# Reordering the end of a sliding-window attention and soft-MoE kernel: products, a spread and sums moved between the last products, results copied by two engines, first outputs of one token

## The chip, the cores and the metric

The kernel runs on one core of a Trainium2 chip. The core has five engines that run their own instruction streams and meet through semaphores: TensorE (PE, with its weight loads as PEld), VectorE (DVE), ScalarE (ACT), GpSimd (POOL) and SyncE (SP). Data moves between HBM and SBUF through 16 DMA engines, which all queues share. Matmul results land in PSUM, 8 banks of 512 fp32 columns in each partition. The metric is device time in microseconds, the median of several executions; a profiled execution also gives a span and a trace.

## The reference

Attention over a causal window of 64 positions, for 8 batches, 8 heads, 576 positions and head size 64, gives `x` (4608 tokens of 512 columns). A soft mixture of experts follows, with 8 experts of 4 slots each:

```python
logits = x @ phi                          # 4608 x 32
d = softmax(logits, axis=0)               # over the tokens
slot_input = (d.T @ x).reshape(8, 4, 512)
h = relu(slot_input[e] @ w1[e])           # 512 -> 1024, for each expert e
slot_out[e] = h @ w2[e]                   # 1024 -> 512
c = softmax(logits, axis=1)               # over the 32 slots
out = c @ slot_out                        # 4608 x 512, fp32
```

## The kernel before

The order of all work is written out by hand (`tc.manual_schedule()`): each engine executes its instructions in the order of the program text, and the framework adds the semaphore waits that the data and the buffers need. Attention is computed in 32 steps of two heads. While it runs, the dispatch softmax is accumulated, and the weights are loaded and cast by transfers on the GpSimd queue. The outputs go out through transfers on SyncE's queue.

What the change touches is the end, from about 147 us on.

- `first` (L871) and `turn_hidden` (L886) compute the hidden layer of the experts in two groups of four: group 0 is experts 0 to 3, group 1 experts 4 to 7. `second_first` (L893) multiplies group 0 by its second weights into one PSUM bank, `op`, over all 512 columns.
- For group 1 the 512 output columns are done in two halves, `d` = 0 and 1, of `DH` = 256 columns. `second(d)` (L899) adds experts 4 and 5, whose weights are there early; `second_last(d)` (L906) adds experts 6 and 7. The weights of experts 6 and 7 are loaded last, half by half (`load_half`, L165): for each `d`, two transfers of expert 6 (tile `w`) and then two of expert 7 (tile `w2h`), each with four of the eight chunks `fc`. `j` = 2 is expert 6 and `j` = 3 expert 7.
- The result of a half is copied from `op` to SBUF, to `osb` (shown by its buffer's name, `qb`), and is then the moving operand of the output products.
- The combine weights of each batch lie in `ct_all` in a compact form. `spread(b, copy)` (L716) widens them: five products into the PSUM tile `rp`, then one copy of 576 columns to `ct4` (shown as `v`) by the engine given. `ct4[k]` holds batches 2k and 2k+1. `sums(k)` (L731) makes the softmax denominators of `ct4[k]` by nine products, again into a tile `rp`, and VectorE writes their reciprocals, `rcs`. The pool `psr` has one buffer for `rp`, so a spread or sums waits until the reader of the `rp` before is done.
- `give(k, e0, ne, c0, nc_)` (L951) makes one piece of output: for the batches 2k and 2k+1, of the 9 tokens that each partition holds, those from `e0` to `e0+ne`, and the columns `c0` to `c0+nc_`. For each token there is one product into a PSUM tile `cp` (L961), and then one scaled copy into an SBUF buffer `ob`, by ScalarE (L968) or VectorE (L966). A `cp` is one bank: two tokens of 256 columns or one of 512, with 4 buffers in the pool `pst`. The counter `turn` goes up by one for each tile `cp`, so that the two engines take whole tiles in turn. At the end the piece is issued as one transfer on SyncE (L970). There are 7 buffers for pieces.
- `fill(k, bank)` issues `k` products of 512 columns whose results nobody reads.

The output order is: left half (columns 0 to 255) of batches 0 to 3, right half of the same, and then whole rows of the other four batches, three tokens to a piece. After `second(0)` the program issues `spread(2, act)`, `second_last(0)`, the copy of the first half by ScalarE, the products of `spread(3)`, the pieces `give(0, 0, 2)` and `give(0, 2, 2)`, the copy of `spread(3)` by VectorE, `give(0, 4, 5)`, `second(1)` and `sums(1)`, and so on.

Of the kernel before, what the change touches and what calls it, by code (L numbers as in the profile page):

```python
# [9 lines left out]
FP32 = mybir.dt.float32  # L10
# [8 lines left out]
def kernel(  # L19
# [13 lines left out]
    D, NSLOT = moe_phi.shape  # L33
# [129 lines left out]
    DH = D // 2  # L163
# [13 lines left out]
    def w2_at(e, d, fc):  # L177
        return w2_t[e][d][fc] if e == last else w2_t[e][fc][:, DH * d:DH * d + DH]
# [367 lines left out]
    def cb_exp(b):  # L546
        ec = pw.tile([128, 6, 32], FP16, name="ec", tag="ec") if b < B - 1 else \
            lh[:, 3:5, :].rearrange("p i x -> p (i x)")[:, 0:192].rearrange("p (i s) -> p i s", s=32)
        nc.scalar.activation(ec[:, :, :], lgs.pop(b)[:, :, :], AF.Exp)
        cbs[b] = ec  # L550

    def cb_turn(b):
        nc.vector.transpose(ct_all[:, b, :], cbs.pop(b)[:, :, :].rearrange("p i s -> p (i s)"))
# [138 lines left out]
    def fill(k, bank):  # L692
        for _ in range(k):
            nc.tensor.matmul(bank, ident_h[:, :], wm[:, 0:4, :].rearrange("p c x -> p (c x)"),
                             start=True, stop=True, skip_group_check=True)
# [15 lines left out]
    def spread(b, copy, rp=None):  # L711
        if rp is None:
            rp = psr.tile([128, 1024], FP32, name="rp", tag="rp")
        for t in range(5):
            w = 128 if t < 4 else 64
            nc.tensor.matmul(rp[:, 128 * t:128 * t + w], ss4[:, min(t, 3), :],  # L716
                             ct_all[:, b, 128 * (t // 4):128 * (t // 4) + w], start=True, stop=True,
                             skip_group_check=True)
        copy(out=ct4[b // 2][:, :, 64 * (b % 2):64 * (b % 2) + 64],
             in_=rp[:, 0:S].rearrange("p (x e) -> p e x", e=NE))  # L720
# [7 lines left out]
    def sums(k):  # L728
        rp = psr.tile([128, 1024], FP32, name="rp", tag="rp")
        for e in range(NE):  # L730
            nc.tensor.matmul(rp[:, e:e + 1], ct4[k][:, e, :], one[:, :], start=True, stop=True, skip_group_check=True)  # L731
        nc.vector.reciprocal(rcs[:, k, :], rp[:, 0:NE])

    b, p = B - 1, NP - 1
# [119 lines left out]
    psr = ctx.enter_context(tc.tile_pool(name="psr", bufs=1, space=bass.MemoryType.PSUM))  # L854
# [11 lines left out]
    ops = [op[:, 256 * d:256 * d + 256] for d in range(2)]  # L866
# [32 lines left out]
    def second(d):  # L899
        for fc in range(NFC):  # L900
            for j in range(2):
                nc.tensor.matmul(ops[d][32 * j:32 * j + 32, :], hT[1][:, fc, 32 * j:32 * j + 32],
                                 w2_at(4 + j, d, fc), start=False, stop=False, skip_group_check=True)


    def second_last(d):  # L906
        for j in (2, 3):
            for fc in range(NFC):
                i = fc % 4
                nc.tensor.matmul(ops[d][32 * i:32 * i + 32, :], hT[1][:, fc, 32 * j:32 * j + 32],  # L910
                                 w2_at(4 + j, d, fc), start=False, stop=(j == 3 and fc >= 4), skip_group_check=True)

    act, dve = nc.scalar.copy, nc.vector.tensor_copy
# [23 lines left out]
    cb_turn(b - 2)  # L937
    second(0)
    cb_exp(b)
    spread(2, act)  # L940
    cb_turn(b - 1)
    cb_turn(b)
    osb = qbs[0][:, 0:4, :, :].rearrange("p i l x -> p (i l x)")
    pex.close()
    obs = [w1_t[e, 0][:, 0:3, :].rearrange("p c f -> p (c f)").bitcast(FP32) for e in range(NRES)]
    pst = ctx.enter_context(tc.tile_pool(name="pst", bufs=4, space=bass.MemoryType.PSUM))


    turn, piece = 0, 0

    def give(k, e0, ne, c0, nc_):  # L951
        nonlocal turn, piece
        ov = out[2 * S * k:2 * S * k + 2 * S, :].rearrange("(p e) d -> p e d", e=NE)
        ob = obs[piece % NRES][:, 0:ne * nc_].rearrange("p (e d) -> p e d", d=nc_)
        piece += 1
        n1 = 512 // nc_
        for i0 in range(0, ne, n1):
            n_ = min(n1, ne - i0)
            cp = pst.tile([128, n1, nc_], FP32, name="cp", tag="cp")
            for i in range(n_):  # L960
                nc.tensor.matmul(cp[:, i, :], ct4[k][:, e0 + i0 + i, :], osb[:, c0:c0 + nc_],  # L961
                                 start=True, stop=True, skip_group_check=True)
            for i in range(n_):
                rc = rcs[:, k, e0 + i0 + i:e0 + i0 + i + 1]
                if turn % 2:
                    nc.vector.tensor_scalar(out=ob[:, i0 + i, :], in0=cp[:, i, :], scalar1=rc, scalar2=None, op0=ALU.mult)  # L966
                else:
                    nc.scalar.activation(ob[:, i0 + i, :], cp[:, i, :], AF.Copy, scale=rc)  # L968
            turn += 1
        nc.sync.dma_start(out=ov[:, e0:e0 + ne, c0:c0 + nc_], in_=ob)  # L970

    def spread_product(b):
        rp = psr.tile([128, 1024], FP32, name="rp", tag="rp")
        spread(b, lambda out, in_: late.append((out, in_)), rp)


    second_last(0)
    act(out=osb[:, 0:DH], in_=ops[0])
    late = []
    spread_product(3)  # L980
    give(0, 0, 2, 0, DH)
    give(0, 2, 2, 0, DH)
    dve(out=late[0][0], in_=late[0][1])
    give(0, 4, 5, 0, DH)
    second(1)
    sums(1)
    give(1, 0, 3, 0, DH)
    give(1, 3, 3, 0, DH)
    give(1, 6, 3, 0, DH)
    second_last(1)  # L990
    act(out=osb[:, DH:D], in_=ops[1])
    give(0, 0, 2, DH, DH)
    give(0, 2, 3, DH, DH)
    give(0, 5, 4, DH, DH)
    spread(4, act)
# [41 lines left out]
```

## Time and profile before

| what | value |
|---|---|
| median of 3 runs | 190.79 us (190.56 to 190.94) |
| profiled execution, time | 190.64 us |
| profiled execution, span | 188.9 us |
| PE, PEld, DVE, ACT, POOL busy, share of the span | 84%, 61%, 76%, 69%, 57% |
| output transfers on SyncE's queue | 18, of 256 to 768 KB |
| first and last output transfer issued | 160.60 us, 179.43 us |
| last compute instruction of the program ends | 177.4 us |

The page shows busy shares, and the span in 40 slices of 4.7 us; in these, a digit is a busy share in tenths, and GB/s what the DMA engines moved. The DMA share is the mean over 16 engines of the time that their packets took; where packets overlap it is above 1. In a timeline a line is a group of like instructions: start and length in us, engine, line of the program, operation, tiles, count, and in brackets the idle time before the group and what ended it.

### The profile page before, as it was taken

The numbers are of one execution on the slowest core, as the hardware profiler recorded it, in microseconds if no ns is written. First come the engines' busy times: TensorE is split into PE (matmuls) and PEld (weight loads), VectorE is DVE, ScalarE is ACT, GpSimd is POOL, SyncE is SP. The second block draws the span as 40 slices with busy tenths as digits, with TensorE's granted clock in tenths as the row PEclk, the third lists the DMA queues.
The fourth block names the chain that finished last, engine by engine and source line by source line (L and its number), as shares of the span: only waits on it lengthen the run. The fifth ranks groups of instructions, "written<-read, shape, count | busy, mean of one in ns | idle before, by whom it ended". The sixth has DMA issues, their size and how long they took to land.

```text
span 188.9 us, 6819 instructions
## 1 busy us (share of the span) xinstructions
PE 158.0 (84%) x2890; PEld 114.8 (61%) x2890; DVE 144.0 (76%) x356; ACT 129.7 (69%) x250; POOL 107.9 (57%) x181
## 2 busy tenths in 40 slices
PE   7786989989999999999999999889888996868300
PEld 2455878866877778687687868756743463543000
DVE  5888688888888899889889889988876251989500
ACT  5486787887787789688778778964764353589300
POOL 7956876967769496598948839581347450000000
PEclk9999999999999999999999999999997899999855
DMA  5999999999999999999999999999999999999995
GB/s 159 221 184 184 187 182 225 176 221 182 185 223 178 217 187 185 216 186 203 205 179 208 195 197 200 207 214 192 214 208 198 208 196 196 282 355 352 408 418 243
DMA packets 63726, 41.46 MB, mean 220 GB/s; under 512 B 38976, under 2 KB 59984, under 8 KB 62800
## 3 DMA queue, kind: packets, MB, share of 16 engines
q0 software_dynamic: 56672, 30.35, 116.6%
q1 hardware_dynamic: 7024, 10.68, 16.4%
q8 instruction: 22, 0.36, 0.7%
q14 instruction: 8, 0.07, 0.1%
HBM read 61.93 MB, written 9.44 MB: 378 GB/s over the span
## 4 chain that ended last, share of the span: by engine, by line
PE 33%; DVE 29%; DMA 21%; issue 5%; ACT 3%; POOL 2%; DVEq 0%; SPq 0%; ACTq 0%
DMA w<-in_moe_w_dram 16%; DVE m L402 8%; DVE x_b L470 5%; PE a_m L397 5%; PE a_s L423 3%; PE a_s L429 3%; PE a_q L351 3%; PE a_k L351 3%; DVE rt L416 3%; PE a_m L393 3%; DMA out_dram<-w 2%; DVE m L412 2%; DMA w<-in_q_dram 2%; PE a_k L484 2%; PE a_v L408 2%
## 5 line engine op out<-in xcount | busy, mean ns | idle before, releaser
L402 DVE TENSOR_REDUCE m<-a_m 128x8 f16<-128x1024 f32 x32 | 39.1, 1221 | 0.0
L436 ACT ACTIVATE pt<-a_s 128x1024 f16<-128x1024 f32 x32 | 32.8, 1025 | 7.3 <-PE a_s L429 7.1
L370 POOL COPY qb<-qp 64x288 int32<-64x288 int32 x54 | 22.9, 425 | 23.9 <-ACT qp L367 20.4
L488 ACT COPY xt<-a_k 128x576 f16<-128x576 f16 x28 | 17.9, 640 | 12.5 <-PE a_k L484 12.4
L470 DVE TENSOR_TENSOR x_b<-a_v,rc 128x640 f16<-128x640 f32 x31 | 25.6, 825 | 1.1
L362 ACT ACTIVATE kT<-a_k 128x576 f16<-128x576 f16 x31 | 20.3, 655 | 0.6 <-PE a_k L351 0.5
L416 DVE TENSOR_TENSOR rt<-a_v,kind 36x256 f16<-36x256 f32 x30 | 12.8, 428 | 10.0 <-PE a_v L415 9.4
L397 PE MATMUL a_m<-kT,qb 128*128 128x128 f16 x256 | 19.8, 220 | 0.3 <-ACT qb L381 0.3
L191 POOL DMA_DIRECT2D v<-in_v_dram x16 | 20.0, 1250 | 0.0
L423 PEld LDWEIGHTS <-kT 128*128 128x128 f16 x288 | 18.6, 98 | 1.8 <-issue 1.4
L423 PE MATMUL a_s<-qb,kT 128*128 128x128 f16 x256 | 19.5, 219 | 0.0
L397 PEld LDWEIGHTS <-qb 128*128 128x128 f16 x256 | 14.5, 98 | 7.9 <-issue 5.0
L367 ACT ACTIVATE qp<-a_q 128x576 f16<-128x576 f16 x27 | 18.0, 666 | 1.9 <-PE a_q L351 1.8
L429 PE MATMUL a_s<-rt,lh 128*128 128x256 f16 x128 | 19.2, 273 | 0.0
L351 PE MATMUL a_q<-ident_h,qs 96*64 96x96 f16 x384 | 15.4, 207 | 4.3 <-DVE a_q L248 1.5
L966 DVE TENSOR_SCALAR w<-cp,rcs 128x256 f32<-128x256 f32 (+1 forms) x27 | 13.8, 566 | 5.3 <-PE cp L961 5.0
L351 PEld LDWEIGHTS <-qs 96*64 96x64 f16 x384 | 12.5, 109 | 6.4 <-issue 4.8
L460 PE MATMUL a_v<-v,pt 128*64 128x65 f16 x558 | 15.1, 195 | 0.6 <-DVE rt L416 0.4
L968 ACT ACTIVATE w<-cp,rcs 128x256 f32<-128x256 f32 (+1 forms) x27 | 12.8, 547 | 3.0 <-PE cp L961 2.0
L201 POOL COPY v<-v 64x576 int32<-64x576 int32 x16 | 10.6, 665 | 7.3 <-DMA v<-in_v_dram 6.7
L351 PE MATMUL a_k<-ident_h,ks 96*64 96x96 f16 x384 | 14.2, 210 | 0.5 <-ACT ks L114 0.4
L460 PEld LDWEIGHTS <-pt 128*64 128x64 f16 x576 | 13.1, 111 | 1.1 <-issue 0.4
(195 smaller groups left out, 348.0 us busy)
## 6 DMA issues: line engine op xcount, KB each, us to landing
w<-in_moe_w_dram POOLq DMA_DIRECT2D x12, 1024.0 KB, 15.2
v<-in_v_dram POOLq DMA_DIRECT2D x16, 288.0 KB, 12.6
out_dram<-w SPq DMA_DIRECT2D x6, 768.0 KB, 6.9
ks<-in_k_dram POOLq DMA_DIRECT2D x15, 288.0 KB, 13.4
qs<-in_q_dram POOLq DMA_DIRECT2D x15, 288.0 KB, 12.0
out_dram<-w SPq DMA_DIRECT2D x7, 384.0 KB, 4.6
w1h<-in_moe_w_dram POOLq DMA_DIRECT2D x4, 256.0 KB, 13.2
w<-in_moe_w_dram POOLq DMA_DIRECT2D x4, 256.0 KB, 12.4
```

The lines of the kernel that those rows point to most:

```text
L191: nc.gpsimd.dma_start(out=v1s[b % 2][:, c, 0:Dh], in_=v[b].rearrange("h s d -> (h s) d").rearrange("(c p) d -> p c d", p=128)[:, c, :])
L351: nc.tensor.transpose(tq[64 * hf:64 * hf + 64, RP * r:RP * r + RP], src[0:RP, h + hf, Dh * r:Dh * r + Dh], ident_h[0:RP, 0:RP])
L362: nc.scalar.activation(kTs[p % NK][:, 64:64 + S], turned(a_kh), AF.Copy, scale=QKS)
L370: nc.gpsimd.tensor_copy(out=qbs[p % NQ][:, :, :, :].rearrange("p i l x -> p (i l x)").bitcast(mybir.dt.int32) .rearrange("p (i l x) -> p i ...
L397: nc.tensor.matmul(a_m[:, i // 4, 128 * (i % 4):128 * (i % 4) + 128], qblock(p, i), kwindow(p, i), start=False, stop=True, skip_group_chec ...
L402: nc.vector.reduce_max(m.rearrange("p e j -> p j e"), a_m[:, :, :].rearrange("p l (j e x) -> p (l j) e x", e=2, x=128), axis=AXX)
L416: nc.vector.tensor_tensor(out=rts[p % NR][64:100, :].rearrange("p (e x) -> p e x", e=2), in0=t_[64:100, :].unsqueeze(1).broadcast_to([36, ...
L423: nc.tensor.matmul(at(i), kwindow(p, i), qblock(p, i), start=(i % 4 == 0), stop=False, skip_group_check=True)
L429: nc.tensor.matmul(a_s[:, i // 4, 128 * (i % 4):128 * (i % 4) + 256], lh[:, i // 2, :], rt[:, :], start=False, stop=True, skip_group_check ...
L436: nc.scalar.activation(st_pt(p)[:, 0:8, :].rearrange("p i x -> p (i x)"), a_s[:, :, :], AF.Exp, scale=XS)
L460: nc.tensor.matmul(a_v[r0:r0 + 64, hf, 65 * (i // 2):65 * (i // 2) + 65], pt[:, i, 64 * hf:64 * hf + 64], rhs, start=True, stop=True, skip ...
L470: nc.vector.tensor_tensor(out=xbs[b][:, :, 128 * hp:128 * hp + 128].rearrange("p c (l d) -> p l c d", l=2), in0=avv[:, :, :, 0:64], in1=rc ...
```

## The change

The 16 products of `second(1)` move from behind the first pieces to right behind `second(0)`, ahead of `spread(2)`. `second_last` can take work to be issued between its products: before expert 6's chunk 4 the whole of `spread(3)` with its copy on VectorE; before expert 7's chunk 0 two products that nobody reads (`idle(2)`); before expert 7's chunk 4 `sums(1)` and one more such product. The copy of a half's result is split into two copies of 128 columns, the left one by ScalarE and the right one by VectorE (`copy_half`). In `give`, the engines alternate by token instead of by tile. The first piece of each half has one token, and so has the second.

```diff
-    def second_last(d):
+    def second_last(d, between={}):
         for j in (2, 3):
             for fc in range(NFC):
+                if (j, fc) in between:
+                    between[j, fc]()
                 i = fc % 4
                 nc.tensor.matmul(ops[d][32 * i:32 * i + 32, :], hT[1][:, fc, 32 * j:32 * j + 32],
                                  w2_at(4 + j, d, fc), start=False, stop=(j == 3 and fc >= 4), skip_group_check=True)
...
     second(0)
     cb_exp(b)
+    second(1)
     spread(2, act)
     cb_turn(b - 1)
     cb_turn(b)
...
-                if turn % 2:
+                if (turn + i) % 2:
                     nc.vector.tensor_scalar(out=ob[:, i0 + i, :], in0=cp[:, i, :], scalar1=rc, scalar2=None, op0=ALU.mult)
                 else:
                     nc.scalar.activation(ob[:, i0 + i, :], cp[:, i, :], AF.Copy, scale=rc)
-            turn += 1
+            turn += n_
         nc.sync.dma_start(out=ov[:, e0:e0 + ne, c0:c0 + nc_], in_=ob)
 
-    def spread_product(b):
-        rp = psr.tile([128, 1024], FP32, name="rp", tag="rp")
-        spread(b, lambda out, in_: late.append((out, in_)), rp)
-
-
-    second_last(0)
-    act(out=osb[:, 0:DH], in_=ops[0])
-    late = []
-    spread_product(3)
-    give(0, 0, 2, 0, DH)
+
+    def copy_half(d):
+        for i, copy in enumerate((act, dve)):
+            c = slice(128 * i, 128 * i + 128)
+            copy(out=osb[:, DH * d + c.start:DH * d + c.stop], in_=ops[d][:, c])
+
+
+    def idle(k):
+        cp = pst.tile([128, 512], FP32, name="cp", tag="cp")
+        fill(k, cp[:, :])
+
+    second_last(0, {(2, 4): lambda: spread(3, dve), (3, 0): lambda: idle(2), (3, 4): lambda: (sums(1), idle(1))})
+    copy_half(0)
+    give(0, 0, 1, 0, DH)
+    give(0, 1, 1, 0, DH)
     give(0, 2, 2, 0, DH)
-    dve(out=late[0][0], in_=late[0][1])
-    give(0, 4, 5, 0, DH)
-    second(1)
-    sums(1)
+    give(0, 4, 2, 0, DH)
+    give(0, 6, 3, 0, DH)
     give(1, 0, 3, 0, DH)
     give(1, 3, 3, 0, DH)
     give(1, 6, 3, 0, DH)
     second_last(1)
-    act(out=osb[:, DH:D], in_=ops[1])
-    give(0, 0, 2, DH, DH)
+    copy_half(1)
+    give(0, 0, 1, DH, DH)
+    give(0, 1, 1, DH, DH)
     give(0, 2, 3, DH, DH)
     give(0, 5, 4, DH, DH)
     spread(4, act)
```

## The prediction, made before the change was run

> **What bounds the kernel now.** I read the page's 40 slices first, then stretches around the first output, then the timeline of the tail, then the rows of the spread tile. In the slices the transfer engines are busy from end to end, while the compute engines stand still in the last two and more:
>
> ```profile
> PE   7786989989999999999999999889888996868300
> ...
> DMA  5999999999999999999999999999999999999995
> GB/s 159 221 184 184 187 182 225 176 221 182 185 223 178 217 187 185 216 186 203 205 179 208 195 197 200 207 214 192 214 208 198 208 196 196 282 355 352 408 418 243
> ```
>
> So the end is a queue draining: about 196 GB/s while weights come in, 355 to 418 while the 9.44 MB of output go out. Compute matters only where it lets that queue run dry. The stretches (columns: us, busy time of PE, PEld, DVE, ACT, POOL with counts, granted clock, DMA share, GB/s) show where that happens:
>
> ```profile
> 160.00:160.50 0.50, 0.30 (x3) 0.12 (x2) 0.50 (x2) 0.50 (x3) 0.00 (x0) 1.00 1.44 194
> ...
> 161.00:161.50 0.50, 0.50 (x14) 0.46 (x12) 0.50 (x2) 0.50 (x2) 0.00 (x0) 1.00 0.98 131
> 161.50:162.00 0.50, 0.50 (x16) 0.29 (x11) 0.50 (x2) 0.17 (x1) 0.00 (x0) 1.00 1.32 290
> ...
> 163.00:163.50 0.50, 0.41 (x3) 0.19 (x2) 0.50 (x3) 0.41 (x2) 0.00 (x0) 1.00 0.86 247
> 163.50:164.00 0.50, 0.50 (x14) 0.34 (x16) 0.50 (x2) 0.23 (x1) 0.00 (x0) 1.00 1.06 365
> ```
>
> At 161 us weights run out and output has not begun; at 163 a little is missing again. In full-rate terms that is some 0.4 us lost: 131 of 196 over 0.5 us is 0.17, 247 of 356 is 0.15, the rest crumbs. That 0.4 us is all that an earlier first output can win. What sets the first output is in the timeline (start, length, engine, line):
>
> ```profile
> 156.02 0.28 PEld L716 LDWEIGHTS <-v 128*128 128x128 f16 x5 [0.21 <-issue]
> 156.03 0.43 PE L716 MATMUL rp<-ct_all,v 128*128 128x128 f16 x5
> ...
> 157.18 0.29 PE L910 MATMUL op<-w2h,hT 128*32 128x256 f16 x4 [0.39 <-DMA w2h<-in_moe_w_dram]
> ...
> 158.50 0.29 PE L910 MATMUL op<-w2h,hT 128*32 128x256 f16 x4 [1.03 <-DMA w2h<-in_moe_w_dram]
> ...
> 158.84 0.37 ACT L978 CAST qb<-op 128x256 f16<-128x256 f32 x1 [1.71 <-PE op L910]
> ```
>
> TensorE waits 0.39 and 1.03 us for the last weights, finishes the first half's products at 158.50, ScalarE copies the result, and the first output transfer is issued at 160.60 (SyncE's first L970). Its bytes move 0.91 us later: the first output packet starts at 161.51.
>
> **The change, part by part, to the first output.** Everything below counts from the profiled execution: span 188.9, time 190.64, which is 0.15 under the median 190.79; I add the sum to the median.
>
> *Second half's first products, moved.* The 16 products of L902 ran from 160.82 until the next work at 161.80: 0.98 us. They now stand ahead of the second spread, so L716 starts at 157.00 instead of 156.03. Alone this is hidden by the 1.42 us of waits.
>
> *The third spread and the sums, moved between the last products.* The spread tile rp has one buffer, so each spread waits until the copy before it is done, and sums(1) reads what both copies wrote. The same chain of spread, spread, sums stands later in this trace, on the same tile:
>
> ```profile
> 166.55 0.41 PE L716 MATMUL rp<-ct_all,v 128*128 128x128 f16 x5
> ...
> 167.69 0.41 PE L716 MATMUL rp<-ct_all,v 128*128 128x128 f16 x5 [0.40 <-ACT v L719]
> ...
> 168.95 0.38 PE L731 MATMUL rp<-one,v 128*128 128x1 f16 x9 [0.53 <-DVE v L719]
> ```
>
> That is 1.14 + 1.26 = 2.40 us from the first spread to the sums, with the first copy on ScalarE and the second on VectorE, as the change has it. Begun at 157.00, the spread issues at 158.14 and the sums at 159.40. The products of the early chunks and idle(2) (two 512-column products, 0.22 apart as three of them in 0.81 us at 172.04 show) fit inside that chain. Behind the sums come their own 0.24 us (161.80 to 162.04 before) and idle(1), 0.22: the last four products go at 159.86, not 158.50. **+1.36 us.** All that TensorE does afterwards, the copies and the first outputs are queued behind this wait. VectorE has nothing else queued behind its spread copy but the reciprocal (about 159.8 to 160.0, free in time).
>
> *The result copied by two engines.* ScalarE takes 373 ns for 256 columns and 639 for 576, so 0.27 us for 128; VectorE 474 and 758, so about 0.36. Both halves lie in one bank of PSUM. Whether the two read it together is not in the trace; both ends: together, 0.36 us against 0.37, so -0.01; one after the other, 0.27 + 0.06 for the signal + 0.36 = 0.69, so **+0.32**. I take the second, since waits here already go by the bank: at 159.73 ScalarE starts the first token 0.36 us after the bank's second product (0.11 behind the first at 159.27), though it needs only the first. (That row names a weight load as releaser; the spacing fits the product.) No row shows ScalarE and VectorE reading one single-buffered PSUM tile at once.
>
> The Trainium skill speaks against the parallel copy too: "PSUM — Partial Sum Buffer", section "PSUM bank collisions raise a hardware error", says that two engines in one bank and one group of 32 partitions are an error even if both only read, so that compilers put a dependency between them. By that rule the copy costs +0.32, without it -0.01; the trace has no such pair to confirm it.
>
> *First outputs of one token.* Before, 1.33 us from first product to issue (159.27 to 160.60), holding two tokens of ScalarE 0.37 apart. Now the tile has one product: 0.36 + one token of 0.475 + 0.03 to the issue = 0.86. **-0.47.** The tokens after it alternate between the engines inside a bank: one at a time per bank, but in different banks at once, about 0.5 us a pair (0.256 MB), against 0.74 us that the output rate of 356 takes for it. Worst case, no overlap, 1.0 us a pair; SyncE's issues, 0.50 apart at 160.60 and 161.10, cover most of that.
>
> *Three more transfers.* 0.5 us each on SyncE's queue. The last one is issued at 179.43 and lands 8.5 us later, which covers them; without cover, up to 1.5 us.
>
> *Work gone from behind the first outputs* (second(1), VectorE's 0.75 us copy, sums): it held back the third transfer until 162.29 and so caused the 0.15 us at 163. That is won back below.
>
> Sum: issue of the first output at 160.60 + 1.36 + 0.32 - 0.47 = **161.81** (copies together: 161.48); its bytes at 162.72 (162.39).
>
> **From there to the end.** Weights do not end at once: the 16 landing records of the last load show 11 engines at 160.95 to 162.15 and 5 at 163.13 to 163.81. Records come 0.33 us after the packets, so the 11 run dry at 161.1 on average. Until 162.72 that is 1.6 us on 11 of 16 engines, 1.1 us in all; the first two transfers, 8 packets of 46 ns an engine for each 0.50 us of issue, lose 0.13 twice on those engines, 0.18. So 1.28 lost, against 0.40 before: **+0.88**. If only the total rate counts, this is the price. Lower end: if the 5 late engines set the end, who are never idle, 0. Upper end: if the 11 early ones do, the whole 1.2. I take 0.85, because after the start the rate is 355 in total whether the engines stand far apart (first landings 162.58 to 164.57) or close (172.42 to 173.09): a lost byte is made up by none. 190.79 + 0.85 = **191.6**.
>
> **Rivals.**
> - *Both engines read the bank together.* Bytes at 162.39: 1.27 x 11/16 + 0.18 - 0.40 = +0.65, 191.4. For it: the column halves are disjoint. Against: the waits by bank. 0.15.
> - *The early engines set the end:* +1.2, 192.0. For it: at the end nearly all engines land within 0.3 us of one another. Against: the steady total rate. 0.10.
> - *The late engines set the end, or the delay is hidden:* +0 to +0.3, about 190.9. For it: one engine lands 0.4 us behind the rest in every late transfer, and it may be one of the five. Against: late engines catch up, from 2 us to 0.7, before the end. 0.18. The change would then not do what it says: its earlier start never comes, and nothing is lost.
> - *Faster: the waits do hold the moved work.* If the sums are issued by 158.2, the last products still go at 158.50, and the first output at 160.60 - 0.01 - 0.47 = 160.12; the 11 engines hardly run dry, and the 0.4 us are won: 190.4. It decides if the spread-to-sums chain takes 1.2 us instead of 2.4, or the last weights land 1.3 us later against TensorE. For it: the waits exist, 1.42 us. Against: two copies of 0.64 and 0.75 us in the chain are by themselves longer than that. 0.15.
>
> **How the numbers follow.** The forecast has 0.42. A measurement of this kernel tells 0.2%, 0.38 us, from no change. Slower: 0.42 + 0.15 + 0.10 = 0.67; same 0.18; faster 0.15. The range leaves out the faster case and what lies beyond the early-engine case: 190.7 to 192.1.
>
> **What would show it.** TensorE's sums (L731) at about 159.4 with a wait on VectorE's spread copy; the last products at 159.9; no wait for weights there; VectorE's half copy beginning after ScalarE's ended; the first SyncE issue near 161.8; a stretch from 161.5 to 162.5 with a GB/s below 150. Wrong if the first issue is before 160.6, if the two copies overlap, or if the stretch is empty and the last landing is still at 187.9.

## The result, and the profile after

The changed kernel is slower: 191.78 us median against 190.27 for the kernel before in the same comparison, a ratio of 1.0066 with a 95% interval of 1.0045 to 1.0086. That is +1.26 us (0.86 to 1.64); +0.85 was forecast. The ratios here and below are worked out from all executions of a comparison except those more than 1.5% above the fastest of the same kernel, and so differ a little from the quotient of the two medians (1.0079 here). The profiled execution of the changed kernel has a span of 190.6 us and a time of 192.32, which is 0.5 over its median; that of before had 188.9 and 190.64. Single executions scatter widely in both kernels: 190.75 to 193.2 us changed, 189.82 to 191.81 before.

The slices of the page after. The transfer engines are busy to the end as before, but the five slices that were 282, 355, 352, 408 and 418 GB/s now read 242, 340, 340, 404 and 415:

```profile
DMA  6999999999999999999999999999999999899996
GB/s 170 211 187 183 185 192 212 181 228 175 185 223 182 212 186 186 216 185 214 192 181 214 190 206 195 211 206 202 212 207 190 201 197 190 242 340 340 404 415 254
```

The timeline of the changed kernel, from the second spread to the first output. Here `second(0)` begins at 155.06, the same instant as in the profile of before, so the two can be laid side by side:

```profile
156.90 0.43 PE L716 MATMUL rp<-ct_all,v 128*128 128x128 f16 x5
...
158.06 0.41 PE L716 MATMUL rp<-ct_all,v 128*128 128x128 f16 x5 [0.51 <-ACT v L719]
...
158.51 0.76 DVE L719 CAST v<-rp 128x576 f16<-128x576 f32 x1 [2.92 <-PE rp L716]
...
158.62 0.60 PE L694 MATMUL cp<-wm,ident_h 128*128 128x512 f16 x2
...
159.16 0.29 PE L912 MATMUL op<-w2h,hT 128*32 128x256 f16 x4
...
159.38 0.38 PE L731 MATMUL rp<-one,v 128*128 128x1 f16 x9
...
159.62 0.38 PE L694 MATMUL cp<-wm,ident_h 128*128 128x512 f16 x1
...
159.93 0.29 PE L912 MATMUL op<-w2h,hT 128*32 128x256 f16 x4
...
160.27 0.27 ACT L979 CAST qb<-op 128x128 f16<-128x128 f32 x1 [2.27 <-PE op L912]
160.64 0.29 DVE L979 CAST qb<-op 128x128 f16<-128x128 f32 x1 [0.62 <-ACT qb L979]
160.98 1.32 PE L964 MATMUL cp<-qb,v 128*128 128x256 f16 x9 [0.76 <-DVE qb L979]
...
161.79 7.00 SPq L973 DMA_DIRECT2D out_dram<-w  x9
```

No wait for weights is left. The last four products go at 159.93, 1.43 us later than before, and 1.55 us after their weights landed (158.38 by the landing records). They stand behind the unread product at 159.62, the sums at 159.38 and, further back, the third spread at 158.06, which waited for ScalarE's copy of the second.

The row of the sums shows no wait, although they read what VectorE's spread copy wrote. That copy ended at 159.27. In the profile of before, sums went 0.05 us behind such a copy (168.90 to 168.95), which would be 159.32 here. But right ahead of the sums, at 159.16, stand four products of expert 7, put off by the two unread products at 158.62, so TensorE itself reached the sums only at 159.38. The copy and TensorE's own queue thus allow the sums within 0.06 us of one another. Without the three unread products the last four would have gone at about 159.56, an estimate from these rows (159.32 and the 0.24 us of the sums): so some 0.37 of the 1.43 us is the unread products' share. No run took them out alone.

The two copies of the result follow one another: VectorE's row names ScalarE's copy as what it waited for. The first output is issued at 161.79 instead of 160.60.

The stretches around it (columns as in the prediction):

```profile
161.50:162.00 0.50, 0.48 (x5) 0.28 (x4) 0.39 (x1) 0.50 (x2) 0.00 (x0) 1.00 0.95 141
162.00:162.50 0.50, 0.30 (x3) 0.12 (x2) 0.34 (x1) 0.50 (x3) 0.00 (x0) 1.00 0.45 61
162.50:163.00 0.50, 0.30 (x2) 0.19 (x2) 0.50 (x3) 0.50 (x2) 0.00 (x0) 1.00 0.88 225
163.00:163.50 0.50, 0.49 (x5) 0.29 (x4) 0.50 (x3) 0.22 (x1) 0.00 (x0) 1.00 0.33 75
163.50:164.00 0.50, 0.26 (x3) 0.09 (x1) 0.50 (x2) 0.14 (x1) 0.00 (x0) 1.00 0.55 182
164.00:164.50 0.50, 0.23 (x3) 0.19 (x2) 0.21 (x1) 0.50 (x2) 0.00 (x0) 1.00 0.79 246
...
166.00:170.00 4.00, 1.94 (x17) 1.47 (x17) 2.83 (x7) 2.73 (x8) 0.00 (x0) 1.00 1.03 341
```

The last of these stretches in the profile of before:

```profile
166.00:170.00 4.00, 2.75 (x32) 1.91 (x32) 3.30 (x9) 3.59 (x10) 0.00 (x0) 1.00 1.06 355
```

In terms of the full rates (196 GB/s for weights, 355 for output) some 1.4 us are lost from 161.5 to 164.5, against 0.4 before. Two losses were not in the prediction: a second hole at 163 to 164, behind SyncE's second issue, which took 0.98 us instead of 0.42; and a lower rate long after, 341 GB/s in the stretch from 166 to 170 where the profile of before has 355. At the 4% between them, the 11 us to 175 lose another 0.45. That makes 1.0 + 0.45 of the 1.7 us by which the spans differ. The packet records of the two traces say where the difference arises: the first 0.5 MB of output has left 1.29 us later than before, the first 4.7 MB (the half rows) 1.77 us later, and the first 9.3 MB 1.78 us later. So the start and the half rows lose all of it, and the whole rows nothing.

### The profile page after: what moved, and what is told of

The parts are those of the page before. It is cut to its first block, busy times and chain, and to the rows that moved or that the text cites. A ratio compares the mean times of both kernels' runs of the same rounds, so it can differ in the third digit from the quotient of the medians.

```text
span 190.6 us, 6837 instructions
## 1 busy us (share of the span) xinstructions
PE 160.3 (84%) x2893; PEld 116.0 (61%) x2893; DVE 145.0 (76%) x358; ACT 129.5 (68%) x250; POOL 107.3 (56%) x181
## 5 line engine op out<-in xcount | busy, mean ns | idle before, releaser
L397 PEld LDWEIGHTS <-qb 128*128 128x128 f16 x256 | 14.6, 98 | 7.5 <-issue 5.6
L964 PE MATMUL cp<-qb,v 128*128 128x256 f16 (+1 forms) x54 | 12.3, 338 | 3.6 <-DVE qb L979 2.1
## 6 DMA issues: line engine op xcount, KB each, us to landing
w<-in_moe_w_dram POOLq DMA_DIRECT2D x12, 1024.0 KB, 15.7
```

Source lines behind the costliest of these rows:

```text
L397: nc.tensor.matmul(a_m[:, i // 4, 128 * (i % 4):128 * (i % 4) + 128], qblock(p, i), kwindow(p, i), start=False, stop=True, skip_group_chec ...
```

## The experiments

The theory: the sums' wait for two copies holds the last products of the first half, so the output starts late, and what the transfer engines idle in the meantime is not made up. Rivals: the small pieces, the split copy or the alternation inside a bank cost the time, or a late start is hidden. The ratios are to the kernel before, run on the same chip in the same comparison, with 95% intervals. Executions scatter by 1 us and more here, so that ten to twelve of each changed version leave intervals 0.3 to 0.7% wide; the profiles tell more than the ratios, but each shows one execution.

**The delay alone.** The kernel before, with eleven unread products ahead of the last four:

```diff
+    cp = pst.tile([128, 512], FP32, name="cp", tag="cp")
+    fill(11, cp[:, :])
+    second_last_end(0)
     act(out=osb[:, 0:DH], in_=ops[0])
```

(`second_last_end` issues the products of expert 7's chunks 4 to 7, which `second_last(0)` then leaves to it.)

> The kernel before, with eleven products that nobody reads put ahead of the last four products of the first half, and nothing else changed: the last products go at about 159.9 instead of 158.5, as in the changed kernel. The first output should be issued at 160.60 + 1.4 = 162.0. If the total rate of the transfer engines counts (my theory), the 11 early engines lose 1.4 us more each, 0.95 us in all: 191.2 against 190.27 for the kernel before, ratio 1.005. If the early engines set the end: +1.4, ratio 1.0074. If the late engines set it: ratio 1.000.

Measured: 1.0045 (1.0021 to 1.007). In the timeline the last products go at 160.15, behind the eleven, and 1.42 us after their weights landed (158.73):

```profile
157.67 2.55 PE L694 MATMUL cp<-wm,ident_h 128*128 128x512 f16 x11
160.15 0.29 PE L916 MATMUL op<-w2h,hT 128*32 128x256 f16 x4
```

The stretches of the same run have a hole at 162, and 339 GB/s afterwards, as in the changed kernel:

```profile
162.00:163.00 1.00, 0.73 (x11) 0.50 (x12) 1.00 (x3) 1.00 (x4) 0.00 (x0) 1.00 0.45 60
163.00:164.00 1.00, 1.00 (x22) 0.75 (x19) 1.00 (x4) 0.32 (x1) 0.00 (x0) 1.00 0.91 271
166.00:170.00 4.00, 2.55 (x25) 1.86 (x24) 3.38 (x9) 3.27 (x8) 0.00 (x0) 1.00 1.04 339
```

A delay of the first output by itself, with the old pieces, copies and alternation, brings the loss and the low rate. That a late start is hidden is refuted.

**Without the work between the last products.** The changed kernel, with the spread's products behind the last ones, its copy and the sums behind the first pieces:

```diff
-    second_last(0, {(2, 4): lambda: spread(3, dve), (3, 0): lambda: idle(2), (3, 4): lambda: (sums(1), idle(1))})
+    second_last(0)
     copy_half(0)
+    rp3 = psr.tile([128, 1024], FP32, name="rp", tag="rp")
+    late = []
+    spread(3, lambda out, in_: late.append((out, in_)), rp3)
...
     give(0, 4, 2, 0, DH)
+    dve(out=late[0][0], in_=late[0][1])
     give(0, 6, 3, 0, DH)
+    sums(1)
```

> The changed kernel with the work taken out from between the last products: the third spread's products stand behind the last products, its copy and the sums behind the first pieces, no unread products. second(1) stays early, the copy by two engines and the one-token pieces stay. Theory: the last products go at 158.5 and the first output is issued at 161.79 - 1.43 = 160.4; nearly the whole loss goes: ratio to the kernel before 1.000 (0.998 to 1.002). Rival, that the loss comes from the small pieces and the alternation inside a bank: still 1.004 or more.

Measured: 0.9977 (0.995 to 1.0003): the loss is gone. Split copy, alternation by token, small pieces and the early `second(1)` are all still there, so none of them makes it. The changed kernel itself was not in this comparison; two close relatives below were, with ratios of 1.0012 and 1.0031. In the timeline the last products wait for weights again:

```profile
158.20 0.29 PE L912 MATMUL op<-w2h,hT 128*32 128x256 f16 x4 [1.00 <-DMA w2h<-in_moe_w_dram]
...
159.26 1.63 PE L964 MATMUL cp<-qb,v 128*128 128x256 f16 x9 [0.40 <-DVE qb L979]
```

And in the stretch behind the start the rate is back at 357 GB/s (the granted clock stands at 0.50 here, third from the right):

```profile
166.00:170.00 4.00, 3.20 (x17) 2.26 (x17) 2.67 (x7) 2.48 (x6) 0.00 (x0) 0.50 1.06 357
```

**Spread or sums?** Only the sums and the unread products taken out; the spread and its copy stay between:

```diff
-    second_last(0, {(2, 4): lambda: spread(3, dve), (3, 0): lambda: idle(2), (3, 4): lambda: (sums(1), idle(1))})
+    second_last(0, {(2, 4): lambda: spread(3, dve)})
...
     give(0, 6, 3, 0, DH)
+    sums(1)
```

> The changed kernel with only sums(1) and the three unread products taken out from between the last products, and sums(1) put behind the first half's pieces of batches 0 and 1; the third spread and its copy on VectorE stay between the last products. Theory: it is the sums' wait for VectorE's copy that holds the last products, while the spread itself fits the wait: the last products go within 0.2 us of the weights' landing (158.5 to 158.7), the first issue 1.86 us behind them; ratio 0.997 to 1.000. Rival, the spread's own wait for ScalarE's copy is enough: the last products go 0.5 us or more behind the weights, ratio 1.003.

Measured: 0.9998 (0.997 to 1.0026). The products still wait 0.92 us for weights, with the spread ahead of them:

```profile
158.25 0.29 PE L912 MATMUL op<-w2h,hT 128*32 128x256 f16 x4 [0.92 <-DMA w2h<-in_moe_w_dram]
159.30 1.63 PE L964 MATMUL cp<-qb,v 128*128 128x256 f16 x9 [0.76 <-DVE qb L979]
```

In this execution `second(0)` began at 153.59, 1.5 us earlier than in the profile of before, so that alone doesn't prove the spread free. The distance does: from `second(0)` to the last products the changed kernel needs 4.87 us, with the spread alone in between 3.57, in the run below where the weights were there first. With 155.06 that gives 158.6, beside weights that land at 158.5. It is the sums, with the unread products around them, that don't fit; the two were not taken apart, beyond the estimate above. The ratio doesn't decide: it overlaps that of the changed kernel in the same comparison, which follows.

**The changed kernel again, and three versions of its details.** The changed kernel on another chip:

> The changed kernel once more, beside the kernels below and the kernel before on the same chip: ratio 1.005 to 1.008 if the loss is that of the first measurement.

Measured: 1.0022 (0.999 to 1.0053), less than the 1.005 to 1.008 expected, and not clear of no change; single times go from 190.62 to 193.61. So the size of the loss in time rests on the first comparison and on the bare delay. The timeline of the profiled execution, one of the longer ones (193.25), has the whole chain 1.47 us later, with the same distances:

```profile
158.37 0.43 PE L716 MATMUL rp<-ct_all,v 128*128 128x128 f16 x5
...
161.40 0.29 PE L912 MATMUL op<-w2h,hT 128*32 128x256 f16 x4
```

One copy by ScalarE instead of two, first run and second:

```diff
-        for i, copy in enumerate((act, dve)):
-            c = slice(128 * i, 128 * i + 128)
-            copy(out=osb[:, DH * d + c.start:DH * d + c.stop], in_=ops[d][:, c])
+        act(out=osb[:, DH * d:DH * d + DH], in_=ops[d])
```

> The changed kernel with each half's result copied by ScalarE alone, 256 columns in one copy. Theory: the copy takes 0.37 us instead of 0.27 + 0.37 with the signal between, the first output is issued 0.25 to 0.3 us earlier, at 161.5; ratio to the kernel before 1.005 instead of 1.0066. If the two copies were as good as one: 1.0066.

> The changed kernel with the result copied by ScalarE alone, once more and beside the changed kernel itself: the first run gave 1.0012 against 1.0066 measured on another chip, which is 1 us, three times the 0.29 us that its profile shows between the last products and the first issue. Theory: 0.0015 below the changed kernel of this same call, and no more.

Measured: 1.0012 (0.9985 to 1.0039), then 0.9996 (0.9973 to 1.0019) beside the 1.0022 of the changed kernel. The distance from last products to first issue is 1.58 and 1.57 us instead of 1.86: 0.29 for the split, as foretold. The ratio of the first run, 1.0012, is further from the 1.0066 of the first comparison than 0.29 us explains, and the second run suggests that the comparison made the rest: beside the changed kernel itself the difference is 0.0026, and 0.0015 was expected, well inside the intervals.

Alternation by tile as before (`turn % 2`, `turn += 1`):

> The changed kernel with the engines alternating by tile again instead of by token. Theory: the start is nearly the same (first issue at 161.8, the second within 0.1 us), and since the output queue is the bound afterwards, the ratio to the kernel before stays within 0.001 of 1.0066. Rival: the waits inside a bank starve the queue between 163 and 175, where the profile of the changed kernel shows 340 GB/s instead of 355: then 0.4 us come back, ratio 1.0045.

Measured: 1.0031 (0.9998 to 1.0064). The rate from 166 to 170 stays at 340 GB/s, so the waits inside a bank don't make it low; the ratio doesn't decide.

**Parts of the change alone, and faster versions.** `second(1)` early, alone; first pieces of one token, alone; and both together:

```diff
     second(0)
     cb_exp(b)
+    second(1)
...
-    give(0, 0, 2, 0, DH)
+    give(0, 0, 1, 0, DH)
+    give(0, 1, 1, 0, DH)
     give(0, 2, 2, 0, DH)
...
-    second(1)
     sums(1)
```

> The kernel before with the 16 products of second(1) moved to right behind second(0), and nothing else. Theory: the 0.98 us lie inside TensorE's waits of 1.42 us for the last weights, so the last products still go at 158.5 and the first output at 160.6; the third transfer is issued up to 0.5 us earlier, and the queue no longer runs thin at 163: at most 0.15 us won, ratio 0.999 to 1.000. Rival: the early products push the last ones too: 1.002 or more.

> The kernel before with first outputs of one token each, and nothing else. Theory: the first issue comes 0.47 us earlier against the last products (1.63 us behind them instead of 2.10), and 0.1 to 0.3 us of the 0.4 us of idle transfer engines go: ratio 0.999. Rival, the cost of small transfers: the second issue stalls as in the changed kernel (0.98 us instead of 0.42), and the gain is lost: 1.000 to 1.002.

> The parts of the change that lie off the chain to the first output, alone: second(1) early and first outputs of one token; the copy by ScalarE alone, the alternation by tile, the third spread's copy and the sums behind the first pieces as in the kernel before. Theory: first issue 1.63 us behind the last products, no thin stretch behind it, 0.3 us of the 0.4 won: ratio 0.998 to 0.999. If nothing can be won before the last weights land: 1.000.

Measured: 1.002 (0.9998 to 1.0042), 1.0007 (0.999 to 1.0025) and 0.9995 (0.9979 to 1.001). The early products do hide: the last ones still go at 158.26, behind a wait of 1.03 us for weights. One token brings the first issue 1.57 us behind the last products instead of 2.09, as foretold, and the combined version loses under 0.1 us from 161 to 164 instead of 0.4. None of this can be told from no change in the time. The timeline of the combined version, up to the first output products:

```profile
158.69 0.29 PE L910 MATMUL op<-w2h,hT 128*32 128x256 f16 x4 [1.01 <-DMA w2h<-in_moe_w_dram]
...
159.46 1.32 PE L962 MATMUL cp<-qb,v 128*128 128x256 f16 x9
```

The same with the last three tokens of batches 2 and 3 as whole rows (`give(1, 6, 3, 0, D)` in place of two pieces of half rows):

> As the run before, and the last three tokens of the batches 2 and 3 are given as whole rows behind the second half's last products, instead of a left piece ahead and a right piece behind. Theory: 0.79 MB move at the 415 GB/s of whole rows instead of 355, 0.3 us less, and 15 left tokens (5.5 us of transfers from about 161) still cover the time until the second half's first output: ratio 0.996 to 0.998. Rival: the right half's first pieces come too late, the queue runs dry near 166: 1.000 or more.

Measured: 0.999 (0.9973 to 1.0006), between the theory and its rival, and not clear of no change. And the changed kernel without the sums between, with one copy and the alternation by tile:

> As the kernel with the sums taken out, and besides one copy by ScalarE and the alternation by tile: first issue 1.57 to 1.63 us behind the last products. Theory: all of the 0.4 us of idle transfer engines are won: ratio 0.997 to 0.999, the fastest kernel of all. Rival: as an earlier start of this kind brought nothing that could be told (0.9995), 1.000.

Measured: 0.9976 (0.9948 to 1.0004). The timeline of its profiled execution, which was its longest (192.65), has `second(0)` as late as 156.36; there the last products follow 3.57 us behind, at 159.93, without waiting:

```profile
158.21 0.43 PE L716 MATMUL rp<-ct_all,v 128*128 128x128 f16 x5
...
159.82 0.39 PE L912 MATMUL op<-w2h,hT 128*32 128x256 f16 x8
160.69 1.10 PE L964 MATMUL cp<-qb,v 128*128 128x256 f16 x7 [0.47 <-ACT qb L977]
```

No version is faster than the kernel before beyond its interval; 0.9976 and 0.9977 come nearest.

## Why the prediction was right, point by point

*Chain to the last products: right.* Forecast and measured: second spread 157.00 and 156.90, third 158.14 and 158.06, sums 159.40 and 159.38, last products 159.86 and 159.93. The later spread-spread-sums rows of the profile before were a fair price list. The loss hangs on this step: it goes when the work between the products goes, and a bare delay of the same length brings it. One sign did not come: a wait of the sums on VectorE's spread copy. The prediction let the unread products fit inside the chain; in fact two of them, with expert 7's first products behind them, kept TensorE busy until just after the copy had ended, so that the right time of the sums is partly luck. The unread product behind the sums cost 0.31 us (159.62 to 159.93), not 0.22.

*The split copy: right.* One after the other, 0.27 + 0.10 for the signal + 0.29; forecast 0.27 + 0.06 + 0.36. The rival of both engines in one bank together is out. The rule on bank collisions in the Trainium skill ("PSUM — Partial Sum Buffer", section "PSUM bank collisions raise a hardware error") has two readers of a bank kept apart; the trace agrees, VectorE's copy waiting for ScalarE's and beginning 0.10 us after its end (160.54 to 160.64). The error itself shows in no run here.

*First issue: right.* Forecast 161.81, measured 161.79; bytes at 162.72, measured 162.66.

*From there to the end: right in kind, too small, in two terms.* The forecast of 191.6 lies near the median of 191.78 partly by luck, as the kernel before was at 190.27 in this comparison and not at 190.79; the change itself, +0.85, was mis-sized. The prediction had 1.28 us lost, 1.1 of it up to the first bytes and 0.18 behind. Measured are some 1.4, divided otherwise: some 0.6 up to the first bytes (the eleven early engines had their last weights 0.4 us later than in the profile of before, at 162.0 on average) and 0.8 behind, most of it behind SyncE's second issue of 0.98 us, which the prediction took at 0.50. The other is the sentence that after the start "the rate is 355 in total whether the engines stand far apart or close", so that a lost byte is merely not made up. It is 341 after the late start. From 166 to 170 the six profiles whose first bytes came after 162 show 339 to 344, the eight earlier ones 345 to 357. From 170 to 174 the line is less clean: the six have 337 to 341, but four of the eight have 339 to 342 too. In the two profiles side by side the late start cost more than its idle time: 1.15 us in the first bytes went with 1.7 us in the span. The case in which the early engines set the end, at the top of the range, was nearer than thought (+1.2 beside +1.26 measured), though not for its reason: from the second output transfer on, which lands by 164.7, at least 15 of the 16 engines of the changed kernel finish within 0.3 us of one another, so that none is early any more. That engines in step move data more slowly than engines apart would fit; it was not tested.

*Faster, if the last weights landed 1.3 us later against TensorE:* how late they land against TensorE does vary, and the prediction's 0.15 for this case came from one profile. The fourteen profiled executions, each with the time that the granted TensorE clock stood at 0.50 between 143 and 151 us, the start of `second(0)`, the landing of the last products' weights, the last products themselves, their distance from `second(0)`, and the first issue:

| kernel | clock at 0.50 | `second(0)` | weights landed | last products | distance | first issue |
|---|---|---|---|---|---|---|
| before | 3.4 | 155.06 | 158.46 | 158.50 | 3.45 | 160.60 |
| before with the delay | 0 | 154.42 | 158.73 | 160.15 | 5.73 | 162.25 |
| changed | 3.4 | 155.06 | 158.38 | 159.93 | 4.87 | 161.79 |
| changed, again | 6.8 | 156.53 | 158.68 | 161.40 | 4.87 | 163.26 |
| changed, by tile | 3.4 | 154.56 | 157.72 | 159.44 | 4.87 | 161.30 |
| changed, one copy | 3.4 | 155.50 | 159.00 | 160.37 | 4.87 | 161.94 |
| changed, one copy, again | 0 | 154.32 | 158.70 | 159.19 | 4.87 | 160.77 |
| without work between | 0 | 153.80 | 158.16 | 158.20 | 4.40 | 160.06 |
| sums out | 0 | 153.59 | 158.21 | 158.25 | 4.66 | 160.10 |
| sums out, one copy | 6.8 | 156.36 | 158.02 | 159.93 | 3.57 | 161.50 |
| second(1) alone | 0 | 153.78 | 158.22 | 158.26 | 4.48 | 160.36 |
| one token alone | 0 | 153.55 | 158.26 | 158.30 | 4.75 | 159.87 |
| second(1) and one token | 0 | 154.69 | 158.65 | 158.69 | 4.00 | 160.26 |
| whole rows | 3.4 | 154.82 | 158.86 | 158.91 | 4.09 | 160.48 |

TensorE reaches `second(0)` anywhere from 153.55 to 156.53, while the last weights land at 157.72 to 159.00. In the kernel before the weights decide, and TensorE's lateness is swallowed. With the sums between, the distance is 4.87 in all five profiles: there TensorE decides, and every lateness goes on to the output. The moved work would fit only where the weights land 4.87 us or more after `second(0)` begins. In none of the fourteen do they: the nearest are 4.71 (one token alone) and 4.62 (sums out), and the five profiles with the work in place have 2.15 to 4.38. So the faster case was out of reach in every profiled execution, though sometimes by a little only.

Most of what sets TensorE's arrival stands in the clock records, which show half the clock in some executions of the stretch ahead of `second(0)` and not in others. The same stretch in `changed, again`, `before` and `one token alone` (third from the right, the granted clock):

```profile
143.00:150.00 7.00, 6.39 (x36) 2.38 (x40) 3.30 (x13) 1.52 (x7) 5.66 (x8) 0.51 1.07 199
143.00:150.00 7.00, 6.63 (x57) 2.89 (x57) 3.13 (x13) 1.93 (x6) 5.50 (x8) 0.76 1.07 203
143.00:150.00 7.00, 6.53 (x80) 3.10 (x81) 3.69 (x13) 2.51 (x6) 5.96 (x9) 1.00 1.08 202
```

From the first product of L716, at 140.1 to 141.6 us in all fourteen, to `second(0)` it takes 12.7 to 13.4 us in the seven profiles without the low clock, 14.4 to 14.6 in the five with 3.4 us of it, and 15.7 to 16.0 in the two with 6.8 us. The profiles of before and of the changed kernel, compared above, both have 3.4 us of it. Why the clock falls in some executions of one program stays open. This could explain why the changed kernel scattered more than the kernel before in the second comparison (190.62 to 193.61 beside 189.66 to 192.18) and why its ratio was 1.0066 once and 1.0022 the other time; with one profiled execution in each it is not shown.

## What to carry to other kernels

Work put into a wait on a transfer must fit it as a chain: its products, plus the copies on other engines that it waits for, plus the signals between; 1.4 us of wait did not hold 2.4 us of spread, copy, spread, copy, sums. Products that nobody reads are not free there either, if they stand in the order behind which the waited-for products go. Such a wait is also a buffer between two streams whose timing differs by a microsecond or more from one execution to the next (up to 3 us for TensorE and 1.3 us for the weights here), and filling it to the brim takes the buffer away. In this program VectorE's copy waited for ScalarE's copy from the same bank of PSUM, so splitting a copy by columns inside a bank made it 0.29 us longer.

## What the hardware showed beyond that

Among the first four output transfers, SyncE's issue took 0.37 to 0.45 us, but in ten of the fourteen profiles one of them took 0.52 to 1.54 us. Every time it ended 0.37 to 0.41 us after the one 16 KB packet of the instruction queue that falls there, and which itself took 0.93 to 1.45 us (161.91 to 162.87 in the changed kernel, the issue ending at 163.24). In the other four none of the first four issues was held, though in two of them (before, and one token alone) an issue falls inside the packet. What decides it is open, and that the packet is the cause was not tested. The Trainium skill ("Runtime: NRT & Kernel Launch", section "Instruction fetch mechanics") has instructions refilled in blocks of 16 KiB at a cost that is mostly hidden; the size agrees with the trace, and if the packet held these issues, the cost here was not hidden.

The granted TensorE clock also stood at 0.50 from 172 to 175 us in the profile of the changed kernel, and from 160 to 174 us in that of the run without work between. That execution took 190.91 us, beside a median of 191.01 for the kernel before in the same comparison: behind the first outputs no loss from the low clock shows.
